# A Strassen operand moved from GpSimd to VectorE in small steps, and Sinkhorn steps and weight subtractions kept in different feature tiles

## The chip, the cores and the metric

The kernel runs on one core of one Trainium2 chip. The metric is the device time of one execution, in microseconds (us). Five engines work side by side, each in its own program order: TensorE (PE, with its weight loads PEld), VectorE (DVE), ScalarE (ACT), GpSimd (POOL) and SyncE (SP, which issues most DMAs).

## What is computed

Three layers in float32, one behind the other:

```
x   = mLSTM attention(q, k, v, gates)                 # 1536 tokens x 320
P   = exp(x @ w_gate - max)                           # 1536 x 8 experts
8 times: P /= row sums; P /= column sums; P *= N / E  # Sinkhorn
x1  = sum over e of P[:, e] * (relu(x @ w1[e]) @ w2[e])      # moe, every expert for every token
out = gate * (relu(x1 @ v1[e*]) @ v2[e*])             # moe2, one expert e* for each token
```

Precision is kept by splitting each float32 matrix into a high part (fp32r, a rounded copy) and a low part (the difference): `xh`, `xl`, `w1h`, `w1l`, `w2h`, `w2l`, `hh`, `hl`. A product is the sum of high-high, high-low and low-high matmuls.

## The kernel before

The first moe layer is a list of 25 items, written out by hand in `moe1`; an item is one expert on one block of tokens. Tokens lie in blocks 0, 1 and 2 of 512. Items 0 and 1 are expert 0 on the halves of block 0; items 2 to 7 are experts 1 to 6 on block 0; items 8 to 21 are experts 0 to 6 on blocks 1 and 2 in turn; items 22 to 24 are expert 7 on the three blocks. The attention layer is spread into items 0 to 3 by a counter of units (`bg_early`), so its twelve token tiles are computed between the matmuls of block 0.

Items 0 to 7 and 22 to 24 have a first stage of eight *feature tiles* (`s1_unit`, eight matmuls of 512 columns each into one of two PSUM banks named `s`). When the eight are done, ACT takes the relu (`hh`, L707) and DVE the low part (`hl`, L708); only then may the feature tile after next write that bank. The second stage (`s2_mm`, L713 to L715) has four token tiles of four pieces (six matmuls each); the last piece of a token tile is followed by an eviction on DVE (L742, or L740 where an accumulator is first written), which frees one of two banks.

Items 8 to 21 replace the first stage by Strassen's scheme with seven products (`s1_seven`). For these, each token block needs operands made once: the four combinations `th` with low parts `tl`, and a stacked remainder `ts`. `make_x(b)` makes them for blocks 1 and 2. The weight's combinations are made on POOL (`make_sums`, L561 to L567, into the tiles `sums` and `sumt`) and then split by ACT and DVE (`make_w`).

Three more streams run beside the matmuls. `split_chunk` turns a loaded piece of weight (`raw`, four buffers) into high part (ACT, L476) and low part (DVE or POOL, L482), and then lets SP issue the next load into the freed buffer; chunks 0 to `DVE_CHUNKS - 1` have the low part on DVE. `sinkhorn` is a generator whose sixteen half steps on DVE (L404 to L408, then L411 to L414), with an all-reduce on POOL between them, are taken at every second unit from unit 100. `fold_raw` (in item 5) scales the first four items' outputs by P and adds them up.

All work is recorded in program order; an engine runs its instructions strictly in that order and waits where a semaphore is not yet there.

The lines that give the moments, of the version before:

```
if newe and ft < 3 or n == 0 and ft in (2, 4, 6):          # L781: w2 split behind which feature tiles
    split_chunk()
...
if u % 2 == 1 and slow:                                    # L1379: a Sinkhorn half step
...
if n == EARLY and u % 2 == 1:                              # L1429: a fold step, EARLY = 5
    next(active[0], None)
elif EARLY <= n < SEVEN - 1 and (n, u) >= (EARLY, 2 * NF): # make_x, one step a unit, SEVEN = 8
```

A unit `u` counts two to a feature tile (0 to 15), and then one to a piece of the second stage (16 to 31).

## Time and profile before

| | us |
|---|---|
| three timed runs | 981.46, 984.47, 984.52 |
| median of them | 984.47 |
| the profiled execution's own time | 980.54 |
| its span, first to last instruction | 978.8 |
| busy in that span: PE, DVE, ACT, POOL | 938.5, 627.1, 470.9, 312.1 |

The profiled execution lies 0.9 us below the fastest timed run and 3.9 us below the median. Times of rows are counted from the start of the span. The items that the change touches lie at 198.5 to 229.9 us (item 4), 229.9 to 262.9 (item 5), 262.9 to 295.7 (item 6), 295.7 to 322.7 (item 7) and 322.7 to 351 (item 8, the first with seven products). A PE row's end is modelled: matmuls overlap, so the idle time shown before one is less than the distance that the stall adds between two starts.

### The profile page before, as it was taken

To read this page: it belongs to the slowest core of one execution; us is meant where nothing else is said; L and a number is where in the kernel's file an instruction comes from. 1 tells how busy PE (TensorE), PEld (TensorE's weight loads), DVE (VectorE), ACT (ScalarE), POOL (GpSimd) and SP (SyncE) were. 2 spreads that over 40 slices of the span, in tenths; PEclk is the share of its full clock that TensorE was granted. 3 is DMA by queue.
4 is the path that set the end of the run, shared out by engine and by line. 5 is a ranking of instruction groups with operands and counts; after the bars stand their busy time and mean duration, and the time that the engine had idled before them with its cause. 6 is when DMAs were issued, how large, how long until landed. Compare 5 with 4: busy or idle time off the path is not lost. (4 is left out here: it accounts for less than half of the span.)

```text
span 978.8 us, 17087 instructions
## 1 busy us (share of the span) xinstructions
PE 938.5 (96%) x6387; PEld 870.5 (89%) x6389; DVE 627.1 (64%) x1463; ACT 470.9 (48%) x936; POOL 312.1 (32%) x308
## 2 busy tenths in 40 slices
PE   8899989999989999999999999999999999899995
PEld 5888888877878999999999999999988987678995
DVE  8867765676765747474856747474535569874672
ACT  5655546334465446353646446353432135465662
POOL 3222311002537704225070704321221112225663
PEclk9999999999999999999999999999999999899998
DMA  9724431223233304031210304021270035587440
GB/s 196 180 43 109 101 79 44 76 64 119 58 107 86 109 1 130 1 93 38 73 58 5 125 2 130 1 91 50 77 301 28 22 96 148 169 231 226 123 127 20
DMA packets 93719, 91.39 MB, mean 93 GB/s; under 512 B 54845, under 2 KB 82495, under 8 KB 93632
## 3 DMA queue, kind: packets, MB, share of 16 engines
q1 hardware_dynamic: 91424, 83.50, 30.3%
q0 software_dynamic: 2208, 6.75, 2.2%
q8 instruction: 52, 0.85, 0.4%
q14 instruction: 35, 0.29, 0.1%
HBM read 86.29 MB, written 4.76 MB: 93 GB/s over the span
## 5 line engine op out<-in xcount | busy, mean ns | idle before, releaser
L713 PE MATMUL s<-w2h,hh 128*128 128x320 f32 x768 | 241.6, 315 | 1.1 <-DVE acc L742 1.0
L715 PE MATMUL s<-w2h,hl 128*128 128x320 f32 x768 | 238.8, 311 | 0.0
L714 PE MATMUL s<-w2l,hh 128*128 128x320 f32 x768 | 237.9, 310 | 0.0
L713 PEld LDWEIGHTS s<-w2h,hh 128*128 128x128 f32 x768 | 145.1, 189 | 2.6 <-DVE acc L742 1.6
L714 PEld LDWEIGHTS s<-w2l,hh 128*128 128x128 f32 x768 | 145.2, 189 | 0.6
L715 PEld LDWEIGHTS s<-w2h,hl 128*128 128x128 f32 x768 | 144.8, 188 | 0.7
L707 ACT ACTIVATE hh<-s 128x512 fp32r<-128x512 f32 (+1 forms) x88 | 49.1, 559 | 107.5 <-PE s L706 107.4
L615 PE MATMUL a<-th,w 128*128 128x256 f32 x392 | 100.0, 283 | 0.0
L708 DVE SCALAR_TENSOR_TENSOR hl<-s,hh 128x512 fp32r<-128x512 f32 (+1 forms) x88 | 56.2, 639 | 67.3 <-ACT hh L707 66.8
L615 PE MATMUL a<-ts,wx 96*128 96x256 f32 x336 | 95.3, 284 | 0.0
L478 POOL CAST w2h<-raw 128x960 fp32r<-128x960 f32 (+1 forms) x21 | 21.5, 1024 | 218.0 <-PE s L715 218.0
L742 DVE SCALAR_TENSOR_TENSOR acc<-s,probs,acc 128x320 f32<-128x320 f32 x72 | 39.6, 550 | 75.6 <-PE s L715 75.5
L615 PEld LDWEIGHTS a<-th,w 128*128 128x128 f32 x392 | 74.6, 190 | 0.0
L636 ACT COPY p<-a 128x256 f32<-128x256 f32 x56 | 20.9, 374 | 102.5 <-PE a L615 98.5
L615 PEld LDWEIGHTS a<-ts,wx 96*128 96x128 f32 x336 | 63.7, 189 | 0.0
L615 PE MATMUL a<-tl,w 128*128 128x256 f32 x224 | 63.0, 281 | 0.0
L482 POOL TENSOR_TENSOR w2l<-raw,w2h 128x960 fp32r<-128x960 f32 (+1 forms) x27 | 54.9, 2039 | 20.8 <-ACT w2h L476 19.1
L628 DVE SCALAR_TENSOR_TENSOR hl<-s,hh 128x256 fp32r<-128x256 f32 x112 | 46.8, 418 | 22.9 <-ACT hh L624 22.7
L624 ACT ACTIVATE hh<-a 128x256 fp32r<-128x256 f32 x112 | 43.1, 385 | 37.8 <-DVE a L631 32.3
L628 DVE SCALAR_TENSOR_TENSOR hl<-a,hh 128x256 fp32r<-128x256 f32 x112 | 47.6, 425 | 14.4 <-ACT hh L624 6.3
L247 POOL TENSOR_SCALAR_AFFINE_SELECT W<-W 128x512 f32<-128x512 f32 x24 | 17.7, 741 | 112.3 <-issue 88.9
L624 ACT ACTIVATE hh<-s 128x256 fp32r<-128x256 f32 x112 | 43.3, 387 | 8.3 <-DVE s L631 7.5
(360 smaller groups left out, 2381.6 us busy)
## 6 DMA issues: line engine op xcount, KB each, us to landing
raw<-in_moe_w_dram SPq DMA_DIRECT2D x30, 512.0 KB
raw<-in_moe_w_dram SPq DMA_DIRECT2D x30, 480.0 KB
raw<-in_moe_w_dram SPq DMA_DIRECT2D x39, 320.0 KB
raw<-in_moe_w_dram SPq DMA_DIRECT2D x40, 256.0 KB
wr<-in_moe_w_dram SPq DMA_DIRECT2D x8, 1024.0 KB
w2raw<-in_moe_w_dram SPq DMA_DIRECT2D x12, 640.0 KB
raw<-in_moe_w_dram SPq DMA_DIRECT2D x42, 128.0 KB
q<-in_q_dram SPq DMA_DIRECT2D x12, 160.0 KB
```

Source lines behind the costliest of these rows:

```text
L478: hi.tensor_copy(h, rv)
L482: eng.tensor_tensor(out=l, in0=rv, in1=f32(h), op=ALU.subtract)
L615: pe.matmul(bank, w, x, start=(first and n == 0), stop=(n == 3), skip_group_check=True)
L624: act.activation(out=hh[:, ft, h * HT:(h + 1) * HT], in_=p, func=AF.Relu)
L628: dve.scalar_tensor_tensor(out=hl[:, ft, c], in0=p, scalar=0.0, in1=f32(hh[:, ft, c]), op0=ALU.max, op1=ALU.subtract)
L636: act.copy(out=p1, in_=Bk[j])
L707: act.activation(out=hh[:, ft, 0:n], in_=p, func=AF.Relu)
L708: dve.scalar_tensor_tensor(out=hl[:, ft, 0:n], in0=p, scalar=0.0, in1=f32(hh[:, ft, 0:n]), op0=ALU.max, op1=ALU.subtract)
L713: pe.matmul(p[:, 0:DM], hh[:, ft, ts], w2h[:, ft, :], start=(ft == 0), stop=False)
L714: pe.matmul(p[:, 0:DM], hh[:, ft, ts], w2l[:, ft, :], start=False, stop=False)
L715: pe.matmul(p[:, 0:DM], hl[:, ft, ts], w2h[:, ft, :], start=False, stop=(ft == NF - 1))
L742: dve.scalar_tensor_tensor(out=acc[:, tt, 0:DM], in0=p[:, 0:DM], scalar=probs[:, tt, e:e + 1], in1=acc[:, tt, 0:DM], op0=ALU.mult, op1=ALU ...
```

## The change

Seven things change together.

1. In `sinkhorn`, the multiplication by N/E and the one by the reciprocal column sums become one instruction.
2. From item 3 on, the three w2 splits stand behind feature tiles 0, 2 and 4 instead of 0, 1 and 2.
3. No Sinkhorn half step is taken in the first eight units of item 4 (its feature tiles 0 to 3); the steps that are left run to the item's last unit.
4. Fold steps in item 5 are taken at every third unit of the first stage and at each of the first eight pieces of the second.
5. `make_x` runs on DVE and ACT alone, in twenty small steps. Block 1's are taken at odd units of items 5, 6 and the start of item 7; block 2's are taken in item 8, two behind each piece of its second stage. Its scratch (`xs`) and `raw_b` lie in the tile `sums`, which therefore is opened early.
6. `DVE_CHUNKS` goes from 39 to 42: item 7's three w2 low parts move from POOL to DVE.
7. `sums` and `sumt` become one tile, and `p1`, `u4`, `u2` become one tile `pu`.

```diff
@@ -410,8 +410,8 @@
-            dve.tensor_scalar_mul(out=cs[:, 0, :], in0=cs[:, 0, :], scalar1=float(N) / E)
-            dve.tensor_tensor(out=probs, in0=probs, in1=cs[:, 0, :].unsqueeze(1).to_broadcast([128, NT, E]), op=ALU.mult)
+            dve.scalar_tensor_tensor(out=probs, in0=probs, scalar=float(N) / E, in1=cs[:, 0, :].unsqueeze(1).to_broadcast([128, NT, E]),
+                                     op0=ALU.mult, op1=ALU.mult)
...
-    DVE_CHUNKS = 39
+    DVE_CHUNKS = 42
...
-        sx["tmp"] = tc.tile_pool(name="stm", bufs=1)
-        p = sx["tmpp"] = sx["tmp"].__enter__()
-        raw_b[0] = p.tile([128, TPB, DM], F32, name="raw_b")
...
         sx["wx"] = p.tile([128, 9, HF], F32R, name="wx")
-        sx["sm"] = p.tile([128, 3, HF], F32, name="sums")
-        sx["st"] = p.tile([128, 3, HF], F32, name="sumt")
...
+        sums = p.tile([128, 6, HF], F32, name="sums")
+        sx["sm"], sx["st"] = sums[:, 0:3], sums[:, 3:6]
+        pu = p.tile([128, 4, HT], F32, name="pu")
+        sx["p1"], sx["u4"], sx["u2"] = pu[:, 0], pu[:, 1], [pu[:, 2], pu[:, 3]]
+        sx["xs"] = sums.rearrange("p m f -> p (m f)").rearrange("p (x t) -> p x t", t=HT)
+        raw_b[0] = sums.rearrange("p m f -> p (m f)")[:, 0:TPB * DM].rearrange("p (t d) -> p t d", d=DM)
...
     def make_x(b):
...
+        w = sx["xs"]
+        xm, tt, xt, tm = w[:, 0:4], w[:, 4:8], w[0:64, 8:10], w[0:64, 10:12]
+        z, z4 = tm[0:32], xm[0:32]
         th, tl, ts = sx["th", b], sx["tl", b], sx["ts", b]
...
+        def sub(o, x, y, op=ALU.subtract):
+            dve.tensor_tensor(out=o, in0=x, in1=y, op=op)
         act.copy(out=tm, in_=two(f32(xh[b][64:128, 2, :])))
-        yield
-        pool.tensor_tensor(out=xm.rearrange("p a h t -> p a (h t)"), in0=f32(xh[b][:, 0:2, :]), in1=f32(xl[b]), op=ALU.add)
...
-        pool.tensor_tensor(out=xt, in0=two(f32(xh[b][0:64, 2, :])), in1=tm, op=ALU.add)
-        yield
-
-        def combine(o, a1, a2, b1, b2, first):
-            return [(o[:, first], a2, a1), (o[:, first + 2], b2, a2), (o[:, first + 1], b2, o[:, first]), (o[:, first + 3], b1, o[:, first + 1])]
-        for o, x, y in combine(tt, xm[:, 0, 0], xm[:, 0, 1], xm[:, 1, 0], xm[:, 1, 1], 0):
-            pool.tensor_tensor(out=o, in0=x, in1=y, op=ALU.subtract)
-            yield
-        act.copy(out=th, in_=tt)
-        act.copy(out=z[:, 0:2], in_=xt[32:64])
-        yield
-        dve.tensor_tensor(out=tl, in0=tt, in1=f32(th), op=ALU.subtract)
-        yield
-        for o, x, y in combine(z, xt[0:32, 0], xt[0:32, 1], z[:, 0], z[:, 1], 2):
-            pool.tensor_tensor(out=o, in0=x, in1=y, op=ALU.subtract)
-            yield
+        sub(xm[:, 0:2], two(f32(xh[b][:, 0, :])), two(f32(xl[b][:, 0, :])), ALU.add)
+        yield
+        sub(xm[:, 2:4], two(f32(xh[b][:, 1, :])), two(f32(xl[b][:, 1, :])), ALU.add)
+        yield
+        sub(xt, two(f32(xh[b][0:64, 2, :])), tm, ALU.add)
+        act.copy(out=z, in_=xt[32:64])
+        yield
+        sub(tt[:, 0:3:2], xm[:, 1:4:2], xm[:, 0:2])
+        act.copy(out=th[:, 0:3:2], in_=tt[:, 0:3:2])
+        yield
+        sub(tt[:, 1], xm[:, 3], tt[:, 0])
+        yield
+        sub(tt[:, 3], xm[:, 2], tt[:, 1])
+        act.copy(out=th[:, 1:4:2], in_=tt[:, 1:4:2])
+        yield
+        sub(z4[:, 0], xt[0:32, 1], xt[0:32, 0])
+        yield
+        sub(z4[:, 2], z[:, 1], xt[0:32, 1])
+        yield
+        sub(z4[:, 1], z[:, 1], z4[:, 0])
+        yield
+        sub(tl[:, 0:2], tt[:, 0:2], f32(th[:, 0:2]))
+        yield
+        sub(tl[:, 2:4], tt[:, 2:4], f32(th[:, 2:4]))
+        yield
+        sub(z4[:, 3], z[:, 0], z4[:, 1])
+        yield
+        parts = [(0, 1, xt[0:32, 0:1]), (1, 3, z), (3, 5, z4[:, 0:2]), (5, 7, z4[:, 2:4])]
         for q in (0, 64):
-            act.copy(out=ts[q:q + 32, 0], in_=xt[0:32, 0])
-            act.copy(out=ts[q:q + 32, 1:7], in_=z)
-            yield
-        dve.tensor_tensor(out=ts[32:64, 0], in0=xt[0:32, 0], in1=f32(ts[0:32, 0]), op=ALU.subtract)
-        dve.tensor_tensor(out=ts[32:64, 1:7], in0=z, in1=f32(ts[0:32, 1:7]), op=ALU.subtract)
-        yield
+            for x0, x1, a in parts:
+                act.copy(out=ts[q:q + 32, x0:x1], in_=a)
+                if q:
+                    sub(ts[32:64, x0:x1], a, f32(ts[0:32, x0:x1]))
+                yield
@@ -778,7 +777,7 @@
                 assert not left_over
                 for ft in range(NF):
                     s1_unit(t0, nt, ft, lambda: bg(n, 2 * ft))
-                    if newe and ft < 3 or n == 0 and ft in (2, 4, 6):
+                    if newe and (ft < 3 if n < EARLY - 2 else ft in (0, 2, 4)) or n == 0 and ft in (2, 4, 6):
                         split_chunk()
             if n == CLASSIC - 1:
-                close_w()
+                close_x()
                 open_late()
             work = make_w() if nxt and nsv else None
+            x2 = make_x(2) if n == SEVEN else None
...
                     f()
+                if n == SEVEN:
+                    for _ in range(2):
+                        next(x2, None)
                 if work is not None:
                     next(work, None)
...
+        MID = sum(2 * NF + 4 * nt for _, nt, _ in ITEMS[:EARLY - 1])
 
         def bg_early(u):
             for g in list(active):
                 if next(g, "end") == "end":
                     active.remove(g)
-            if u % 2 == 1 and slow:
+            if slow and u % 2 == 1 and not MID <= u < MID + NF:
                 if next(slow[0], "end") == "end":
                     slow.pop(0)
...
-                    xs.extend((make_x(1), make_x(2)))
+                    xs.append(make_x(1))
                 return
             if n == EARLY and u == 0:
                 emit_const2()
-            if n == EARLY and u % 2 == 1:
-                next(active[0], None)
-            elif EARLY <= n < SEVEN - 1 and (n, u) >= (EARLY, 2 * NF):
-                if next(xs[0], "end") == "end" and len(xs) > 1:
-                    xs.pop(0)
-                if (n, u) == (SEVEN - 2, 2 * NF + 4 * TPB - 1):
-                    for g in xs:
-                        drain(g)
-            if n == SEVEN - 1 and u == 0:
-                open_w()
+            if n == EARLY and u < 2 * NF + 8:
+                if u >= 2 * NF or u % 3 == 1:
+                    next(active[0], None)
+            elif EARLY <= n < SEVEN and u % 2 == 1 and u >= 7:
+                next(xs[0], None)
+            if n == SEVEN - 1 and u == 7:
+                drain(xs[0])
```

On DVE, in item 4's first feature tiles, before (`hl` marks the end of a feature tile, L482 is a w2 split, L404 to L413 are Sinkhorn):

```order
L708 SCALAR_TENSOR_TENSOR hl<-s_2159,hh 128x512
L482 TENSOR_TENSOR w2l<-raw,w2h 128x960
L404 TENSOR_REDUCE sk<-probs 128x12
L405 TENSOR_SCALAR sk<-sk 128x12
L406 RECIPROCAL sk<-sk 128x12
L407 TENSOR_TENSOR probs<-probs,sk 128x96
L408 TENSOR_REDUCE cs<-probs 128x8
L708 SCALAR_TENSOR_TENSOR hl<-s_2180,hh 128x512
L482 TENSOR_TENSOR w2l<-raw,w2h 128x960
L411 TENSOR_SCALAR cs<-cs 128x8
L412 RECIPROCAL cs<-cs 128x8
L413 TENSOR_SCALAR cs<-cs 128x8
```

On the same engine at the same place after the change:

```order
L707 SCALAR_TENSOR_TENSOR hl<-s_2157,hh 128x512
L482 TENSOR_TENSOR w2l<-raw,w2h 128x960
L707 SCALAR_TENSOR_TENSOR hl<-s_2172,hh 128x512
L707 SCALAR_TENSOR_TENSOR hl<-s_2183,hh 128x512
L482 TENSOR_TENSOR w2l<-raw,w2h 128x960
L707 SCALAR_TENSOR_TENSOR hl<-s_2199,hh 128x512
L707 SCALAR_TENSOR_TENSOR hl<-s_2210,hh 128x512
L482 TENSOR_TENSOR w2l<-raw,w2h 128x640
L404 TENSOR_REDUCE sk<-probs 128x12
L405 TENSOR_SCALAR sk<-sk 128x12
L406 RECIPROCAL sk<-sk 128x12
L407 TENSOR_TENSOR probs<-probs,sk 128x96
```

Split and Sinkhorn half step stood in one feature tile three times; now they meet once, behind feature tile 4.

On ACT, in item 6 before, between the relus (`hh`) of feature tiles 2, 3 and 4 (`ts` is block 1's stacked remainder):

```order
L707 ACTIVATE hh<-s_2753 128x512
L476 CAST w2h<-raw 128x640
L550 CAST ts_2307<-xt 32x256
L551 CAST ts_2307<-z 32x1536
L550 CAST ts_2307<-xt 32x256
L551 CAST ts_2307<-z 32x1536
L707 ACTIVATE hh<-s_2771 128x512
L707 ACTIVATE hh<-s_2786 128x512
```

On ACT in item 6 after the change, from feature tile 3 on:

```order
L706 ACTIVATE hh<-s_2744 128x512
L706 ACTIVATE hh<-s_2756 128x512
L476 CAST w2h<-raw 128x640
L534 CAST th_2281<-sums 128x2x256
L706 ACTIVATE hh<-s_2773 128x512
L706 ACTIVATE hh<-s_2785 128x512
L706 ACTIVATE hh<-s_2797 128x512
```

The four `ts` copies are gone from between the relus; one `th` copy of 512 columns stands there.

On DVE, in item 8's second stage, where there were only the evictions (L740, now L739), after the change:

```order
L739 TENSOR_SCALAR acc<-s_3358,probs 128x320
L519 TENSOR_TENSOR sums<-xh_67,xl_70 128x512 x2
L519 TENSOR_TENSOR sums<-xh_67,sums 64x512
L519 TENSOR_TENSOR sums<-sums 128x2x256
L519 TENSOR_TENSOR sums<-sums 128x256 x2
L519 TENSOR_TENSOR sums<-sums 32x256 x2
L739 TENSOR_SCALAR acc<-s_3402,probs 128x320
L519 TENSOR_TENSOR sums<-sums 32x256
L519 TENSOR_TENSOR tl_2285<-sums,th_2284 128x512 x2
L519 TENSOR_TENSOR sums<-sums 32x256
L739 TENSOR_SCALAR acc<-s_3439,probs 128x320
```

Behind the third eviction stand four more, which make the low rows of `ts`; block 2's whole operand now stands between item 8's evictions and item 9's first products.

## Rows read from the trace of the kernel before

**Rows 1.** The page, part 1: busy us of each engine (share of the span) xinstructions.
```profile
PE 938.5 (96%) x6387; PEld 870.5 (89%) x6389; DVE 627.1 (64%) x1463; ACT 470.9 (48%) x936; POOL 312.1 (32%) x308
```
**Rows 2.** TensorE's waits, first stages of items 4, 5; second of 5; item 6: total, times, longest.
```profile
PE s L698 <- DVE hl L708: 1.9, 3, 1.0
...
PE s L698 <- DVE hl L708: 2.4, 2, 2.2
...
PE s L713 <- DVE acc L742: 1.0, 1, 1.0
...
PE s L698 <- DVE hl L708: 3.1, 2, 2.3
```
**Rows 3.** Timeline of PE, items 4 and 5: start us, duration us, instruction [idle before <-releaser].
```profile
203.51 0.39 PE L705 MATMUL s<-xh,w 128*128 128x512 f32 x1
203.74 0.39 PE L706 MATMUL s<-xh,w 128*128 128x512 f32 x1
205.12 0.50 PE L698 MATMUL s<-xh,w 128*128 128x512 f32 x1 [0.99 <-DVE hl L708]
...
243.88 0.39 PE L698 MATMUL s<-xh,w 128*128 128x512 f32 x1
```
**Rows 4.** Timeline of DVE in item 4.
```profile
203.10 0.24 DVE L404 TENSOR_REDUCE sk<-probs 128x12 f32<-128x96 f32 x1
...
204.38 0.68 DVE L708 SCALAR_TENSOR_TENSOR hl<-s,hh 128x512 fp32r<-128x512 f32 x1
204.98 1.15 DVE L482 TENSOR_TENSOR w2l<-raw,w2h 128x960 fp32r<-128x960 f32 x1
206.04 0.17 DVE L411 TENSOR_SCALAR cs<-cs 128x8 f32<-128x8 f32 x1
...
206.86 0.68 DVE L708 SCALAR_TENSOR_TENSOR hl<-s,hh 128x512 fp32r<-128x512 f32 x1
```
**Rows 5.** Timeline of POOL in item 5: the first instruction of `make_x`.
```profile
235.98 3.09 POOL L531 TENSOR_TENSOR xm<-xh,xl 128x1024 f32<-128x1024 f32 x1
```
**Rows 6.** Timeline of DVE in items 5 and 6.
```profile
236.74 2.69 DVE L724 SCALAR_TENSOR_TENSOR acc<-acc,probs 128x320 f32<-128x320 f32 x1
...
240.68 0.54 DVE L724 SCALAR_TENSOR_TENSOR acc<-raw_b,probs,acc 128x320 f32<-128x320 f32 x1
...
242.92 0.69 DVE L708 SCALAR_TENSOR_TENSOR hl<-s,hh 128x512 fp32r<-128x512 f32 x1 [0.64 <-ACT hh L707]
...
244.77 0.69 DVE L708 SCALAR_TENSOR_TENSOR hl<-s,hh 128x512 fp32r<-128x512 f32 x1 [0.70 <-ACT hh L707]
...
250.16 2.39 DVE L482 TENSOR_TENSOR w<-raw,w 128x1024 fp32r<-128x1024 f32 x1 [0.56 <-ACT w L476]
...
291.31 0.42 DVE L553 TENSOR_TENSOR ts<-xt,ts 32x256 fp32r<-32x256 f32 x1
```
**Rows 7.** Timeline of ACT in item 6.
```profile
269.69 0.40 ACT L550 CAST ts<-xt 32x256 fp32r<-32x256 f32 x1
...
271.80 1.46 ACT L551 CAST ts<-z 32x1536 fp32r<-32x1536 f32 x1
273.28 1.09 ACT L707 ACTIVATE hh<-s 128x512 fp32r<-128x512 f32 x2
```
**Rows 8.** Timeline of POOL in item 7.
```profile
299.35 6.04 POOL L482 TENSOR_TENSOR w2l<-raw,w2h 128x960 fp32r<-128x960 f32 x3 [12.36 <-ACT w2h L476]
...
310.66 1.29 POOL L561 TENSOR_TENSOR sumt<-raw 96x512 f32<-96x512 f32 x1
```
**Rows 9.** Timeline of DVE in items 7 and 8 and at the start of item 9.
```profile
320.63 0.68 DVE L594 TENSOR_TENSOR w<-sums,w 128x512 fp32r<-128x512 f32 x1
...
341.67 0.55 DVE L740 TENSOR_SCALAR acc<-s,probs 128x320 f32<-128x320 f32 x1 [0.51 <-PE s L715]
...
348.71 0.55 DVE L740 TENSOR_SCALAR acc<-s,probs 128x320 f32<-128x320 f32 x1 [2.97 <-PE s L715]
351.48 0.43 DVE L631 TENSOR_TENSOR s<-s,p 128x256 f32<-128x256 f32 x1 [2.22 <-PE s L615]
```

More of the change, by code (lines that the diff above doesn't have):

```diff
@@ L498, in open_x @@
             sx["ts", b] = p.tile([128, 7, HT], F32R, name=f"ts{b}")
-        sx["tmp"] = tc.tile_pool(name="stm", bufs=1)
-        p = sx["tmpp"] = sx["tmp"].__enter__()
-        raw_b[0] = p.tile([128, TPB, DM], F32, name="raw_b")
-    def open_w():
-        sx["tmp"].__exit__(None, None, None)
-        sx["wp"] = tc.tile_pool(name="swp", bufs=1)
-        p = sx["pool"] = sx["wp"].__enter__()
-        sx["wx"] = p.tile([128, 9, HF], F32R, name="wx")
-        sx["sm"] = p.tile([128, 3, HF], F32, name="sums")
-        sx["st"] = p.tile([128, 3, HF], F32, name="sumt")
-        sx["p1"] = p.tile([128, HT], F32, name="p1")
-        sx["u4"] = p.tile([128, HT], F32, name="u4")
-        sx["u2"] = [p.tile([128, HT], F32, name=f"u2{j}") for j in range(2)]
@@ L515, in close_w @@
-    def close_w():
-        sx["wp"].__exit__(None, None, None)
+        sx["wx"] = p.tile([128, 9, HF], F32R, name="wx")
+        sums = p.tile([128, 6, HF], F32, name="sums")
[4 more added lines that the diff above has]
+        raw_b[0] = sums.rearrange("p m f -> p (m f)")[:, 0:TPB * DM].rearrange("p (t d) -> p t d", d=DM)
@@ L517, in close_w, with close_x @@
+    def close_x():
         sx["xp"].__exit__(None, None, None)
     def make_x(b):
-        p = sx["tmpp"]
-        xm = p.tile([128, 2, 2, HT], F32, tag="xm", name="xm")
-        tt = p.tile([128, 4, HT], F32, tag="tt", name="tt")
-        xt = p.tile([64, 2, HT], F32, tag="xt", name="xt")
-        tm = p.tile([64, 2, HT], F32, tag="tm", name="tm")
-        z = p.tile([32, 6, HT], F32, tag="z", name="z")
+        w = sx["xs"]
+        xm, tt, xt, tm = w[:, 0:4], w[:, 4:8], w[0:64, 8:10], w[0:64, 10:12]
+        z, z4 = tm[0:32], xm[0:32]
```

## The prediction

> **What bounds the kernel now.** The page's first part comes first: TensorE is busy for 96% of the span, the next engine for 64% [rows 1]. So only time in which TensorE stands still, or runs matmuls that it need not, can be won, and the change removes no matmul. The waits of TensorE come second, asked for by item. In items 4, 5 and 6 it waits for `hl` (the low part of the relu, on VectorE) in the first stages for 1.9, 2.4 and 3.1 us, and for one eviction in item 5's second stage for 1.0 us [rows 2]; nothing else there. The timeline of PE gives the true size: two matmuls start 0.23 us apart while each is drawn 0.39 us long, so a wait costs 0.16 us more than the idle time shown; 203.74 to 205.12 is 1.38, 0.23 of it normal, so 1.15 for a wait shown as 0.99 [rows 3]. With 0.16 for each of the eight waits, item 4 loses 1.9 + 3 x 0.16 = 2.4, item 5 2.4 + 2 x 0.16 = 2.7 and 1.0 + 0.16 = 1.2, item 6 3.1 + 2 x 0.16 = 3.4: 9.7 us. That is the most that these edits can return here.
>
> The timelines of VectorE and ScalarE then say why `hl` is late. An undisturbed feature tile takes 1.85 us (242.92 to 244.77), and the `hl` at 242.92 ends at 243.61, while the matmul that may then overwrite its bank starts at 243.88 [rows 3, 6]. So there is 0.27 us of slack: whatever delays one `hl` by more stops TensorE two feature tiles later.
>
> **The change part by part.**
>
> Item 4, first stage. `hl` takes a slot of 0.60 us (204.38 to 204.98), a split of 960 columns 1.06 (204.98 to 206.04), the first half of a Sinkhorn step 1.28 (203.10 to 204.38), the second half 0.82 (206.04 to 206.86) [rows 4]. Before, `hl` + split + first half = 2.94 us against a period of 1.85, three feature tiles running: hence the 2.4. After, feature tiles 0 and 2 hold 0.60 + 1.06 = 1.66 and 1 and 3 hold 0.60: all fit. Feature tile 4 holds the short split (640 columns, 1.06 x 2/3 = 0.71) and a first half: 0.60 + 0.71 + 1.28 = 2.59, or 0.74 late, less 0.27 of slack: about 0.5, taken as 0.6 since the split also waits for ScalarE's copy. From there on a half step of 1.28 with `hl` is 1.88, just even. The merged multiplication saves one instruction of 0.17 us (as L411) in each second half, off the path. Gain 2.4 - 0.6 = 1.8; if feature tile 4 came out even, 2.4.
>
> Item 5, first stage. The long wait is the 2.2 of rows 2, and its cause is one row: a fold instruction that took 2.69 us instead of 0.54 [rows 6], started at 236.74 beside the first `make_x` instruction on GpSimd, 235.98 to 239.07 [rows 5]. After the change GpSimd runs no `make_x`, so the fold takes 0.54, and every third unit it stands where no split does, except in feature tile 0. There split and fold still meet as now: the short wait of 2.4 - 2.2 + 0.16 = 0.4 stays. Gain 2.3.
>
> The Trainium skill (SBUF — State Buffer, Who interferes with whom) has a rule for this: a VectorE instruction with two SBUF inputs and a GpSimd instruction that reads SBUF exclude each other, and the second waits for all of the first. The trace agrees: the fold ends 0.4 us after GpSimd's instruction.
>
> Item 5, second stage. A w1 split took 2.39 us [rows 6], beside GpSimd's `make_x`; the next sizes alone are 1.06 for 960 columns [rows 4]. After, VectorE has in the first eight pieces seven folds (0.5 each), three w1 splits (1.06 x 1024/960 = 1.13 each) and an eviction (0.55): 7.4 us, against eight pieces of 0.88 (two evictions eight pieces apart are 348.71 - 341.67 = 7.04 [rows 9]). It is 0.4 behind, and a bank has four pieces to be freed. Gain 1.2.
>
> Item 6. ScalarE makes the four `ts` copies in one piece from 269.69, and the next relu starts at 273.28 [rows 7]: 3.6 us in a period of 1.85. Its `hl` and the next are late, which is the 3.4. After, the fullest feature tile holds on ScalarE a relu, a w2 copy and one `th` copy, on VectorE `hl`, the short split and a subtraction of 256 columns at 0.42 [rows 6]: 0.60 + 0.71 + 0.42 = 1.73. Gain 3.4.
>
> Item 7. Here the change adds work to a stage without waits. Behind feature tile 3 stand three `ts` subtractions of 512 columns (0.68 each alone [rows 9], 0.60 a slot): `hl` + 1.8 = 2.4, or 0.55 late, less 0.27: 0.3 lost. Then the third split, now on VectorE, meets the first weight sum on GpSimd, which waits for the same subtractions because its output overlays their inputs. Its price: alone 0.71; beside GpSimd up to 2.39/1.13 times that, 1.5 [rows 6]. I take half of the difference, 0.4, of which some 0.3 reaches TensorE, since `hl` behind it has just lost its slack. Loss 0.6; bounds 0 (if ScalarE's relu were the later anyway) and 1.7 (both in full, and the next `hl` too).
>
> By the Trainium skill's rule (SBUF — State Buffer, Who interferes with whom, as above) the split would wait out the whole sum that has begun, at most its 1.29 us [rows 8]; with all of that on TensorE the loss in this item would be 1.6 and the sum 7.1. No row shows this pair.
>
> Queued behind that split is SP's load of the last weight quarter. Before, GpSimd's splits ended at 305.39 and the sum that reads this quarter started at 310.66 without a wait [rows 8], so the load lands in under 5.3 us. After, the split ends some 12.7 us into the item and the sum's turn comes at 16.4 (10.6 when the subtractions are done, four sums of 1.29, and 0.6 for contention): 0 to 1.6 us late, before a `make_w` that has some slack. I take 0, and keep 1 as the bound.
>
> Item 8. Block 2's operand is sixteen VectorE instructions, nine of 512 columns (0.60 a slot) and seven of 256 (0.42 less the overlap, 0.34): 7.8 us. They start behind the eviction at 341.67, with two more evictions between (0.92) and about 0.5 for results that are needed at once: done at 342.13 + 9.2 = 351.3. Item 9's first sum on VectorE starts at 351.48 [rows 9], and TensorE reads only the first `ts` row in its first product, at about 350.6; that row is made before the last three, at 349.6. It fits by less than 1 us. Cover: TensorE's second-stage pieces, in which VectorE stands idle for 2.97 us before an eviction [rows 9]. Without it the whole 7.8 would show. I take 0; bounds 0 and a loss of 1.
>
> The rest. Items 3 and 22 have later splits too: in 3 they stand differently among attention's instructions (0, bounds 0.5 either way); in 22 GpSimd does three splits in 6.04 [rows 8] with 1.85 x 3 = 5.5 us left behind the last one's copy: 0. The loads that splits release start up to 3.7 us later, at least a whole second stage ahead of their use. The shared tiles `pu` and `sums` add no wait between parts that do not overlap, since the program's waits in items 10 to 21 are the same as before: 0.
>
> Sum: 1.8 + 2.3 + 1.2 + 3.4 - 0.6 = 8.1 us. Low end: 8.1 - 0.3 (item 4) - 1.1 (item 7) - 1 (load) - 1 (item 8) - 0.5 (item 3) = 4.2; high end: 8.1 + 0.6 + 0.6 + 0.5 = 9.8. Against the profiled execution, 980.54 - 8.1 = 972.4. The timed runs' median lies 3.9 higher, which by itself gives 984.47 - 8.1 = 976.4. I forecast 975, nearer to the second, as medians are compared.
>
> **The rivals.**
>
> Less comes back. Feature tile 4 of item 4, item 7 and the start of item 9 each turn into a wait: gain 4 or less, 977 to 981. For it: three places that fit by under 1 us. Against: each has its own slack, and they would have to fail together.
>
> More comes back. The stalls that go are those of over 2 us; if timed runs have longer ones than the profiled execution (their median is 3.9 higher), 10 to 13 return: 969 to 972. No row shows it.
>
> No change. The edits only move the stalls: VectorE takes over block 1's operand in items 5 to 7, up to 7.8 us as for block 2, and every feature tile that was relieved fills up again: 983 to 985. Against: only in feature tile 4 of item 4 and in 3 of item 7 does the count exceed 1.85.
>
> Slower. Block 2's subtractions in item 8 are stretched as the fold was, by 2.69/0.54 = 5 [rows 6], if GpSimd reads SBUF beside them: 7.8 becomes 39, item 9 waits 30 us, and the time is near 1000. At three times it is 15.6 longer, less 1 of slack and 8.1 of gain: 6.5 slower, 990. The point that decides is a stretch of (8.1 + 1)/7.8 + 1 = 2.2. For it: the next work of GpSimd in program order is item 9's weight sums, which read SBUF. Against: after the change their output overlays block 2's scratch, so they must wait until it has been read; GpSimd should stand idle there.
>
> **How the numbers follow.** The forecast has 0.67 (971 to 978.5, its own range), less 0.13, more 0.06, no change 0.07, slower 0.07. The range 970.5 to 980.5 takes the forecast, most of "less" and half of "more": 0.8. A difference under 0.3%, 2.9 us, is about what a measurement of this kernel cannot tell from none. Faster by more: 0.67 + 0.13 + 0.06 = 0.86; the same 0.07; slower 0.07.
>
> **What the profile after would show.** Right: item 4 with one wait for `hl` of about 0.5 us, item 5 with one of 0.2, item 6 with none; the folds at 0.54 all through; a new wait in item 7 under 1 us; item 9's first product without a wait, and VectorE's last `ts` subtraction about at its start. Wrong: a wait for `ts` or for a weight part at the start of items 8 or 9; subtractions of 512 columns that take over 1 us in item 8; or all this as said and an equal time, which would mean that the waits removed were not on the path.

## The result, and the profile after

| | before | after |
|---|---|---|
| median (lowest to highest), four runs each | 982.97 (979.87 to 984.52) | 972.02 (970.89 to 973.88) |
| ratio, 95% interval | | 0.9894 [0.9861, 0.9928] |
| profiled execution, its span | 980.54, 978.8 | 973.88, 972.2 |

The change is faster by 1.1%, with an interval of 0.7 to 1.4%. Two later comparisons of the same two kernels gave 0.9921 [0.9892, 0.995] and 0.9903 [0.9875, 0.9931]. The forecast was 975 us, from a sum of 8.1 us.

The page's first part of the kernel after, to be laid beside [rows 1]: GpSimd has lost 30 us of work, VectorE has gained only 6, and TensorE, 96% busy as before, has the same matmuls in a shorter span.

```profile
span 972.2 us, 17087 instructions
...
PE 937.0 (96%) x6389; PEld 869.5 (89%) x6389; DVE 633.2 (65%) x1484; ACT 472.4 (49%) x946; POOL 281.8 (29%) x285
```

TensorE's waits of the kernel after, first for items 4 to 6 (196 to 286 us), then for items 7 to 9 (285 to 375 us): total, times, longest.

```profile
PE s L697 <- DVE hl L707: 1.2, 3, 0.7
...
PE s L697 <- DVE hl L707: 0.5, 1, 0.5
PE s L712 <- DVE acc L741: 0.5, 1, 0.5
```

The 8.4 us of waits of [rows 2] have become 1.2, and item 7 has two new ones. To count what a wait costs without the modelled ends, I take the distance between the first matmuls of two items, from the timeline of PE. The last column is a later variant in which TensorE has no wait left in these items (called "early parts" below), so it shows what each item takes undisturbed.

| us | before | after | difference | forecast | undisturbed |
|---|---|---|---|---|---|
| item 4 | 31.49 | 29.51 | -1.98 | -1.8 | 28.80 |
| item 5 | 32.94 | 29.20 | -3.74 | -3.5 | 28.84 |
| item 6 | 32.85 | 29.74 | -3.11 | -3.4 | 29.00 |
| item 7 | 27.00 | 28.60 | +1.60 | +0.6 | 27.10 |
| items 8 and 9 | 42.60 | 42.60 | 0.00 | 0 | 42.61 |
| sum | 166.88 | 159.65 | -7.23 | -8.1 | 156.35 |

So 8.8 us come back in items 4 to 6, and 1.6 are given away in item 7 (1.5 and 2.0 in two later profiles of the changed kernel, where item 7 takes 28.51 and 28.99 us). Outside these items the two profiled executions differ too, in ways that nearly cancel. The execution of before reached item 4 1.8 us later; it has a stretch of 3.4 us ahead of it with the clock at its lower level, which the execution after does not have. Windows of the kernel before (first TensorE's busy time and its matmuls; the granted clock is the third number from the end; 0.50 is the level of 1.2 GHz):

```profile
139.00:140.70 1.70, 1.26 (x10) 1.27 (x11) 0.48 (x3) 0.00 (x0) 0.00 (x0) 1.00 0.86 248
140.70:144.10 3.40, 3.40 (x15) 3.40 (x14) 3.04 (x6) 0.43 (x1) 0.00 (x0) 0.50 0.36 83
```

And from item 22 to the end the execution after takes 2.6 us longer, 271.3 us against 268.7. Two later profiles of the changed kernel take 267.8 and 270.7 us there, so this stretch differs between executions of one program by as much.

### The profile page after: what moved, and what is told of

It is laid out like the page before. It is cut to its first block, busy times and chain, and to the rows that moved or that the text cites. A ratio compares the mean times of both kernels' runs of the same rounds, so it can differ in the third digit from the quotient of the medians.

```text
span 972.2 us, 17087 instructions
## 1 busy us (share of the span) xinstructions
PE 937.0 (96%) x6389; PEld 869.5 (89%) x6389; DVE 633.2 (65%) x1484; ACT 472.4 (49%) x946; POOL 281.8 (29%) x285
## 5 line engine op out<-in xcount | busy, mean ns | idle before, releaser
L635 ACT COPY pu<-a 128x256 f32<-128x256 f32 x56 | 20.9, 374 | 91.8 <-PE a L614 87.6
L482 POOL TENSOR_TENSOR w2l<-raw,w2h 128x960 fp32r<-128x960 f32 (+1 forms) x24 | 48.9, 2036 | 11.0 <-ACT w2h L476 9.3
```

The source lines that it names most:

```text
L482: eng.tensor_tensor(out=l, in0=rv, in1=f32(h), op=ALU.subtract)
```

## The experiments

**The changed kernel again**, with no edit.

> The changed kernel as it is, for a narrower interval and for the spread between executions. Theory (the gain is the 7.3 us of waits that its profile no longer shows in items 4 to 7): ratio near 0.9925, time some 7 us under the kernel before. Rival (the 11 us between the first medians is real and has a further source outside items 4 to 9): ratio near 0.989. If the mean granted clock of the executions differs between the two kernels, the difference beyond 7 us is in stretches at the lower clock level; if it does not, it is elsewhere.

Measured: 974.9 us against 981.31, ratio 0.9921 [0.9892, 0.995]. Items 4 to 7 take 116.96 us (117.05 in the first profile), so the 7 us are a property of the program, as the theory had it. This execution reached item 4 six us later than the other (202.74 against 196.68), and the windows show where: in the first 28 us, while inputs still arrive. The row of this execution, and under it that of the first profile:

```profile
13.00:28.00 15.00, 14.45 (x66) 13.08 (x66) 7.51 (x20) 6.88 (x11) 2.83 (x11) 0.50 1.07 213
```
```profile
13.00:28.00 15.00, 11.65 (x86) 9.78 (x85) 12.98 (x33) 8.93 (x15) 2.84 (x11) 1.00 1.04 211
```

The same 15 us ran at the lower level in one and at the upper in the other: 66 matmuls instead of 86. Items 4 to 9 of these two profiles and of the profile before hold no stretch at the lower level, so the lengths in the table are free of it.

The expectation also asked whether the mean granted clock differs between the two kernels. It hardly does here, 0.9877 for the kernel before and 0.9884 for the changed one, but it spreads between executions, from 0.979 to 0.997, and the time goes with it. An estimate from the 169 timed runs of all the experiments, with a level for each kernel and each set of comparisons and one common slope: a run is 0.68 us longer for each 0.001 that its mean clock is lower. At equal clock, by this fit, the changed kernel is 6.9 us (5.9 to 8.0) faster here and 7.8 (6.2 to 9.3) in the later comparison. Both agree with the 7.2 us of the items, so no second source is needed. The fit was made after the results were known, and it would also take out what a stall costs by lowering the clock.

**Only the moments (edits 1 to 4).** The kernel before, with the merged multiplication and the new moments of splits, Sinkhorn steps and folds; `make_x` stays on GpSimd, in its own scratch.

```diff
...
-            if n == EARLY and u % 2 == 1:
+            if n == EARLY and u < 2 * NF + 8 and (u >= 2 * NF or u % 3 == 1):
                 next(active[0], None)
-            elif EARLY <= n < SEVEN - 1 and (n, u) >= (EARLY, 2 * NF):
+            if EARLY <= n < SEVEN - 1 and (n, u) >= (EARLY, 2 * NF):
```

> The kernel before with the moments alone changed: merged multiplication, w2 splits behind feature tiles 0, 2, 4 from item 3 on, Sinkhorn paused in item 4, fold steps at the new units; the Strassen operand stays on GpSimd and in items 5 and 6. Theory (three separate causes): item 4's wait for hl falls from 1.9 us to about 0.4, item 5 keeps a wait of about 2 us because a fold still runs beside GpSimd's first instruction, its eviction wait stays at 1 us or more, item 6 keeps its 3.1 us; gain 1.5 to 2.5 us. Rival (the moments are all of it): items 4 to 6 without waits over 0.5 us, gain about 7 us.

Measured: ratio 1.0027 [0.9996, 1.0058], and items 4 to 7 in 130.08 us, 5.8 longer than before. Item 4 gained its 2.0 (29.50). Item 5 took 37.78. Its waits (first row), and what stood on VectorE and GpSimd ahead of the longest:

```profile
PE s L713 <- DVE acc L742: 5.5, 2, 5.3
```
```profile
252.72 1.76 DVE L482 TENSOR_TENSOR w<-raw,w 128x1024 fp32r<-128x1024 f32 x1
254.40 3.36 DVE L724 SCALAR_TENSOR_TENSOR acc<-acc,probs 128x320 f32<-128x320 f32 x1
...
258.26 0.55 DVE L742 SCALAR_TENSOR_TENSOR acc<-s,probs,acc 128x320 f32<-128x320 f32 x1
```
```profile
252.41 2.64 POOL L547 TENSOR_TENSOR z<-z 32x256 f32<-32x256 f32 x2
255.02 2.38 POOL L531 TENSOR_TENSOR xm<-xh,xl 128x1024 f32<-128x1024 f32 x1
```

The fold of 0.54 us [rows 6] took 3.36: it ends 0.36 us behind GpSimd's instruction (255.02 + 2.38 = 257.40), and the eviction is queued behind it. Neither gain expected held. The moments alone push the folds into the second stage, where GpSimd runs the operand; edit 4 needs edit 5. Item 7 lost another 2.38 us at an eviction. Rows of GpSimd, of ACT and of VectorE ahead of it:

```profile
315.45 1.29 POOL L563 TENSOR_TENSOR raw<-raw 96x512 f32<-96x512 f32 x1
```
```profile
316.78 1.05 ACT L590 CAST wx<-raw 96x1024 fp32r<-96x1024 f32 x1 [4.74 <-POOL raw L563]
```
```profile
317.86 1.22 DVE L598 TENSOR_TENSOR wx<-raw,wx 32x1024 fp32r<-32x1024 f32 x1 [3.64 <-ACT wx L590]
```

ScalarE's copy waits for a weight sum of GpSimd, VectorE's subtraction for the copy, and the eviction stands behind the subtraction. The sums come late because GpSimd still makes the three w2 low parts, which now stand behind feature tiles 0, 2 and 4: the last one ends 12.2 us into the item, 9.7 before [rows 8]. So edit 2 needs edit 6 as well. Both long waits were followed by a stretch at the lower clock level:

```profile
258.50:261.90 3.40, 3.04 (x11) 3.04 (x12) 1.90 (x3) 0.00 (x0) 0.00 (x0) 0.50 0.00 0
319.90:323.30 3.40, 3.40 (x14) 3.40 (x15) 3.34 (x4) 2.57 (x2) 0.31 (x1) 0.50 0.73 207
```

The 25 matmuls in them start some 0.12 us further apart than at the upper level (0.27 instead of 0.147), so I estimate that 3 of the 5.8 us are the clock's. At equal clock the timed runs are 2.0 us (0.8 to 3.1) slower than before by the fit above.

**The old moments of splits and Sinkhorn** in the changed kernel (edits 2 and 3 undone).

```diff
-                    if newe and (ft < 3 if n < EARLY - 2 else ft in (0, 2, 4)) or n == 0 and ft in (2, 4, 6):
+                    if newe and ft < 3 or n == 0 and ft in (2, 4, 6):
...
-            if slow and u % 2 == 1 and not MID <= u < MID + NF:
+            if slow and u % 2 == 1:
```

> The changed kernel with w2 splits behind feature tiles 0, 1, 2 again and Sinkhorn not paused. Theory: item 4's three waits for hl come back (1.9 us in total as shown, 2.4 lost), item 5 stays under 0.6; item 6's new wait (0.7 us as shown) goes, since the th copy on ScalarE no longer stands behind a split; item 7 loses 0.5 us less; together 0.3 us slower to 0.7 us faster than the changed kernel. Rival (the engine alone matters, not the moments): item 4 without waits, the time that of the changed kernel in every item.

Measured: ratio 0.9944 [0.9913, 0.9975]; items 4 to 7 in 117.81 us, 0.8 longer. Item 4 loses 2.1 us in three waits (2.4 before the change). But the wait of 0.86 us in item 6 is gone, and the eviction wait in item 7 is down to 0.14. By lengths the new moments are worth 1.8 us in item 4 and 0.4 in item 5, and cost 0.7 in item 6 and 0.6 in item 7. The 0.8 lies just outside the range that was expected; the timed runs do not part this variant from the changed kernel (0.9944 against 0.9921, with intervals that overlap).

**A GpSimd instruction beside the folds.** The changed kernel with one sum more, whose result nobody reads, of the size of the old `make_x` instruction.

```diff
             if n == EARLY and u == 0:
                 emit_const2()
+                w = sx["xs"].rearrange("p x t -> p (x t)")
+                pool.tensor_tensor(out=w[:, 1536:2560], in0=f32(xh[1][:, 0:2, :]).rearrange("p a t -> p (a t)"),
+                                   in1=f32(xl[1]).rearrange("p a t -> p (a t)"), op=ALU.add)
```

> The changed kernel with one more GpSimd instruction at the start of item 5: an addition of 1024 columns that reads SBUF twice, as the first instruction of the operand did before; nothing waits for it and nothing reads its result. Theory (an SBUF-reading GpSimd instruction holds up a VectorE instruction with two SBUF inputs): a fold or a split in item 5's first stage takes 1.5 to 2.7 us instead of 0.54 or 1.16, a wait for hl of 1 to 2.2 us comes back in item 5, the time is 1 to 2.3 us longer than that of the changed kernel. Rival (the long fold was late for another reason): all VectorE durations in item 5 as in the changed kernel, no wait over 0.3 us.

Measured: a new wait of TensorE in item 5's first stage, 1.16 us between starts; items 4 to 7 in 118.89 us, which is within what was expected. Of the 1.9 us more, 1.4 are in item 5 and 0.5 at the eviction in item 7. The sum met a split of 640 columns this time, which alone takes 0.83. Timeline of VectorE, then of GpSimd:

```profile
237.69 2.27 DVE L482 TENSOR_TENSOR w2l<-raw,w2h 128x640 fp32r<-128x640 f32 x1
```
```profile
236.82 2.45 POOL L1434 TENSOR_TENSOR sums<-xh,xl 128x1024 f32<-128x1024 f32 x1
```

GpSimd is done at 239.27; with 0.83 behind that the split would end at 240.10, and it ends at 239.96.

**GpSimd beside block 2's operand**: the slower rival made on purpose. Eleven sums that read SBUF, with a result that nobody reads, in item 8's second stage.

```diff
...
+                if n == SEVEN and x == 0:
+                    for _ in range(11):
+                        pool.tensor_tensor(out=sx["dum"], in0=acc[:, t0, 0:DM], in1=acc[:, t0, 0:DM], op=ALU.add)
                 if n == SEVEN:
                     for _ in range(2):
                         next(x2, None)
```

> The changed kernel with eleven GpSimd additions of 320 columns in item 8, which read SBUF twice, start when the first eviction of its second stage is done, and whose result nobody reads. Theory (the forecast's slower rival, built on purpose: GpSimd reading SBUF stretches block 2's subtractions): the subtractions of 512 columns take 1.2 us or more instead of 0.68, those together end 4 to 8 us later, item 9's first products wait 3 to 7 us for ts, items 4 to 7 stay as in the changed kernel; slower than it by 3 to 7 us. Rival (the place has room enough, or the two engines do not hinder each other): durations of 0.4 and 0.68 as in the changed kernel, no wait over 0.3 us at item 9.

Measured: items 8 and 9 in 47.40 us instead of 42.60, ratio 0.9959 [0.9936, 0.9982]. Of VectorE, GpSimd and TensorE's waits in item 8:

```profile
336.33 4.63 DVE L520 TENSOR_TENSOR sums<-sums 128x512 f32<-128x512 f32 x5
```
```profile
333.63 11.63 POOL L802 TENSOR_TENSOR dum<-acc 128x320 f32<-128x320 f32 x11 [9.81 <-DVE acc L740]
```
```profile
PE a L615 <- ACT ts L552: 2.0, 1, 2.0
PE s L713 <- DVE acc L740: 1.5, 1, 1.5
```

Five sums take 4.63 us that take 2.26 in the changed kernel (below), and both an eviction and item 9's first product wait. The loss of 4.8 us lies in the range expected; TensorE's wait for `ts` is shorter than expected (2.0 us instead of 3 to 7), and the eviction has a part of the loss.

**The operand on GpSimd, at the new moments.** Everything of the change stays, but the sums and differences that make `xm`, `xt`, `tt` and `z` are on GpSimd.

```diff
-        sub(xm[:, 0:2], two(f32(xh[b][:, 0, :])), two(f32(xl[b][:, 0, :])), ALU.add)
+        sub(xm[:, 0:2], two(f32(xh[b][:, 0, :])), two(f32(xl[b][:, 0, :])), ALU.add, eng=pool)
...
-        sub(z4[:, 3], z[:, 0], z4[:, 1])
+        sub(z4[:, 3], z[:, 0], z4[:, 1], eng=pool)
```

> The changed kernel with the additions and subtractions of the operand on GpSimd again, at the new moments; its tl and ts rows stay on VectorE. Theory (the engine matters as much as the moment): in item 8 ten GpSimd instructions of 0.7 to 1.3 us make about 9.5 us before the last z, so item 9 waits 3 to 6 us; in items 5 to 7 folds and splits beside GpSimd are stretched and 0.5 to 3 us of waits come back; slower than the changed kernel by 3 to 8 us. Rival (only the moments matter): the same time as the changed kernel within 1 us in items 4 to 9.

Measured: 974.32 us, ratio 0.9916 [0.9883, 0.995]; items 4 to 7 in 116.27 us, 0.8 *shorter* than on VectorE (item 6 has no wait and takes 28.76), items 8 and 9 0.8 longer, of which 0.35 stand in the second profile of the changed kernel too (42.95). My theory fell. The timeline of GpSimd, and one row of VectorE, show why this is not the old picture:

```profile
244.94 2.18 POOL L519 TENSOR_TENSOR sums<-xh,xl 128x512 f32<-128x512 f32 x1 [6.62 <-ACT w L476]
252.91 1.31 POOL L519 TENSOR_TENSOR sums<-xh,xl 128x512 f32<-128x512 f32 x1 [5.79 <-DVE acc L723]
```
```profile
244.25 0.54 DVE L723 SCALAR_TENSOR_TENSOR acc<-sums,probs,acc 128x320 f32<-128x320 f32 x1
```

Before, the first sum started at 235.98, as soon as GpSimd had nothing else to do [rows 5]. Here it starts 9 us later, in the second stage, 0.15 us behind the end of the fold that reads the second token tile of `raw_b` (the view names a copy of ScalarE for this wait, but that ended at 244.55, and GpSimd's queue waited for VectorE until 244.84). The second one waits for a fold (L723) by name: the scratch lies over `raw_b`, which the folds read. A fold still took 1.62 us beside the first sum, but there it had time.

**The same without the shared memory.** As the last kernel, with `raw_b` in other tiles, so that the scratch no longer lies over it.

```diff
...
-        raw_b[0] = sums.rearrange("p m f -> p (m f)")[:, 0:TPB * DM].rearrange("p (t d) -> p t d", d=DM)
+        r3 = pu.rearrange("p m f -> p (m f)")[:, 0:3 * DM].rearrange("p (t d) -> p t d", d=DM)
+        r1 = p.tile([128, DM], F32, name="raw_b3")
+        raw_b[0] = [r3[:, 0], r3[:, 1], r3[:, 2], r1]
...
```

> Like the kernel with the operand's sums on GpSimd at the new moments, except that the four item-3 outputs (raw_b) lie in other tiles (three in pu, one in a new tile), so that the operand's scratch no longer overlays what the folds read. There, GpSimd's first two sums started at 244.94 and 252.91 us, the second behind a fold on VectorE, and items 4 to 7 took 116.3 us. Theory (the shared memory paced GpSimd): without it GpSimd runs the two sums as soon as its small constants are made, at 236 to 242 us, in item 5's first stage; one fold there takes over 1.2 us instead of 0.55, TensorE stands still 0.7 to 1.6 us for hl, items 4 to 7 take 117.0 to 117.9 us. Rival (the place in the program or another wait paces it): the sums stay at 245 and 253 us and the items at 116.0 to 116.6.

Measured: 978.16 us, ratio 0.9954 [0.9926, 0.9981]; items 4 to 7 in 119.73 us, 3.5 longer than with the overlay. Of GpSimd, of VectorE, and TensorE's waits in items 4 to 7:

```profile
236.37 3.17 POOL L521 TENSOR_TENSOR sums<-xh,xl 128x512 f32<-128x512 f32 x2
```
```profile
238.29 1.60 DVE L725 SCALAR_TENSOR_TENSOR acc<-acc,probs 128x320 f32<-128x320 f32 x1
```
```profile
PE s L714 <- DVE acc L743: 2.6, 2, 2.2
PE s L699 <- DVE hl L709: 2.0, 4, 0.9
```

Both sums run at 236 us, the fold beside them takes 1.60 instead of 0.55, and TensorE stands 1.10 us for `hl`: the theory held for the first stage. It was too small by the second stage, where the rest of the operand now meets the folds and an eviction costs 2.35 more.

**The copies apart.** The kernel before, with three steps of nothing behind each pair of `ts` copies, to price item 6's cause by itself.

```diff
             act.copy(out=ts[q:q + 32, 1:7], in_=z)
             yield
+            yield
+            yield
+            yield
```

> The kernel before with three empty steps behind each pair of ts copies, so that the two pairs on ScalarE stand in two different feature tiles; nothing else changes. Theory (item 6's 3.4 us come from 3.6 us of copies in one piece on ScalarE): item 6's wait for hl falls from 3.1 us to 0.5 to 1.5, as each pair of 1.8 us still overfills its tile by 0.5; items 4 and 5 as in the kernel before; gain 1.5 to 2.5 us. Rival (the wait is VectorE's, from the ts subtraction of 1.74 us or from GpSimd beside it): item 6's wait stays at 2.5 us or more.

Measured: item 6 in 29.54 us instead of 32.85, so the four copies in one piece cost 3.3 us: the 3.4 of the prediction, and more than the 1.5 to 2.5 expected here. Item 4 (31.47 us), item 7 (27.21) and the long stand-still of item 5 repeat the one profile that there is of the kernel before. The time moved less: ratio 0.9982 [0.9953, 1.001], items 4 to 7 1.7 shorter. Item 5, which the edit does not touch, took 34.40 instead of 32.94. Windows of this kernel around the long wait in item 5:

```profile
236.00:240.30 4.30, 2.11 (x8) 1.43 (x8) 4.30 (x4) 2.17 (x4) 3.30 (x5) 0.98 0.81 231
240.30:243.50 3.20, 3.19 (x8) 2.52 (x9) 2.21 (x4) 0.00 (x0) 0.00 (x0) 0.50 0.47 145
```

The stand-still itself was as long as in the kernel before (2.34 us), but here the eight matmuls behind it ran at the lower level, 0.43 us apart instead of 0.23, eight times 0.2 us, which is the 1.5 us. In the profile of before the same stretch is at 1.00.

**Early parts.** The changed kernel with its own leftovers moved: splits back behind feature tiles 0, 1, 2 from item 4 on, Sinkhorn paused for six units instead of eight, the folds from unit 7 on, and block 1's operand finished in item 6, so that item 7 starts clean.

```diff
-                    if newe and (ft < 3 if n < EARLY - 2 else ft in (0, 2, 4)) or n == 0 and ft in (2, 4, 6):
+                    if newe and (ft in (0, 2, 4) if n == EARLY - 2 else ft < 3) or n == 0 and ft in (2, 4, 6):
...
-            if slow and u % 2 == 1 and not MID <= u < MID + NF:
+            if slow and u % 2 == 1 and not MID <= u < MID + 6:
...
-                if u >= 2 * NF or u % 3 == 1:
+                if u >= 2 * NF or u >= 7 and u % 2 == 1:
                     next(active[0], None)
-            elif EARLY <= n < SEVEN and u % 2 == 1 and u >= 7:
+            elif EARLY <= n < SEVEN - 1 and u >= 7 and (u % 2 == 1 or n > EARLY and u >= 2 * NF):
                 next(xs[0], None)
-            if n == SEVEN - 1 and u == 7:
+            if n == SEVEN - 1 and u == 0:
```

> The changed kernel with its four left waits taken away: w2 splits behind feature tiles 0, 1, 2 again in items 4 to 7, Sinkhorn and folds only behind feature tile 3 and later, block 1's operand finished in item 6's second stage. Theory (each of these waits comes from two things in one feature tile): the waits of 0.5 in item 4, 0.3 in item 5, 0.9 in item 6, 0.7 and 0.6 in item 7 go; items 4 to 7 take 114 us instead of 117, the time is about 3 us under the changed kernel. Rival (VectorE is full, waits only move): items 4 to 7 take 116 to 118 us, other waits of the same sum appear, most likely in item 6's second stage.

Measured: 971.54 us, ratio 0.9886 [0.985, 0.9923]. Items 4 to 7 take 113.74 us, and the list of TensorE's waits from 190 to 375 us is empty. To see whether that is worth its 3.3 us, it ran once more beside the changed kernel.

> The same kernel as the variant with the weight splits behind feature tiles 0, 1, 2, a shorter pause and block 1's operand done in item 6, beside the changed kernel in the same call. Items 4 to 7 took 113.7 us in its first profile and 117.0 in the changed kernel's. If that is worth 3.3 us in the timed runs too, its ratio to the kernel before lies 0.003 below that of the changed kernel here, near 0.989 against 0.992; if something later gives it back, the two ratios are equal.

> The changed kernel as it is, for the comparison with the variant beside it in this call: a ratio to the kernel before of 0.992 (0.989 to 0.995), items 4 to 7 in 117.0 us.

Measured: 970.4 us, ratio 0.9895 [0.9857, 0.9932], for the variant; 972.84, 0.9903 [0.9875, 0.9931], for the changed kernel. In the two profiles items 4 to 7 take 113.72 and 117.54 us and the spans 968.9 and 972.1, so nothing gives the gain back there. The medians differ by 2.4 us the same way, but the two ratios by only 0.0008, with intervals that overlap almost wholly: taken as they are, the timed runs do not show the variant to be faster than the changed kernel. The mean granted clock of its six runs was lower, though, 0.9878 against 0.9908. At equal clock, by the fit above, it is 3.2 us (1.4 to 5.1) faster, which agrees with the 3.8 of the items, and 10.2 (8.7 to 11.6) and 11.0 (9.5 to 12.5) faster than the kernel before, where the table has 10.5.

## Why the prediction was right, and where its steps were off

**What bounds the kernel** was read rightly: TensorE's waits in items 4 to 6 were on the path, and taking them away shortened the span by their size. The correction for modelled ends was a little small. Against the undisturbed items, items 4, 5 and 6 lost 2.7, 4.1 and 3.9 us before, 10.6 in all, where I had 9.7.

**Item 4** kept one wait at feature tile 7, 0.53 us between starts; forecast 0.6. In "early parts" its splits stand behind feature tiles 0, 1 and 2, as before the change, and it has no wait: the pause of the Sinkhorn steps (edit 3) is enough for item 4's gain, and the later splits (edit 2) are not needed there. **Item 5** kept one of 0.33 (forecast 0.4), and its folds take 0.54 or 0.55; one follows the third split too (237.30 and 238.04), which I had not seen, and costs nothing. The reason I gave, that GpSimd runs no `make_x`, is true of the changed kernel, but it is not what was needed. With the sums on GpSimd the items are just as short as long as the scratch lies over `raw_b`; without that the stalls return. What item 5's part of the gain rests on is *when* the operand is made. In the kernel before, nothing held GpSimd back, and it ran ahead of its place in the program into the first stage. The change holds the operand back twice: on VectorE by its place in the queue, and by the memory that it shares with the folds. The second is enough, also on GpSimd; the first without the second was not tried.

**Item 6.** The term that I took whole, 3.4, returned 3.1 with a wait of 0.86 us left over. I had added up VectorE's load for a feature tile, 1.73, and named ScalarE's three pieces without adding them, and I had left out the handover between the two. Timeline of ACT, then of VectorE, in item 6 of the kernel after:

```profile
267.20 0.62 ACT L534 CAST th<-sums 128x512 fp32r<-128x512 f32 x1 [1.23 <-DVE sums L519]
267.73 1.30 ACT L706 ACTIVATE hh<-s 128x512 fp32r<-128x512 f32 x2
```
```profile
266.01 0.82 DVE L482 TENSOR_TENSOR w2l<-raw,w2h 128x640 fp32r<-128x640 f32 x1
266.75 0.42 DVE L519 TENSOR_TENSOR sums<-sums 128x256 f32<-128x256 f32 x1
268.35 0.69 DVE L707 SCALAR_TENSOR_TENSOR hl<-s,hh 128x512 fp32r<-128x512 f32 x1 [1.18 <-ACT hh L706]
```

The split stands ahead of the subtraction, the `th` copy waits for the subtraction, and the relu stands behind the copy: ScalarE is idle for 1.23 us, and `hl` comes at 268.35. With the third split two feature tiles earlier (old moments, early parts) this wait is gone, and also with the subtraction on GpSimd, where no split stands ahead of it.

**Item 7** is the mis-sized term: 0.6 lost by forecast, 1.60 measured. Its first part has the size that I gave, 0.69, but partly by luck. All of it is from the three `ts` subtractions (1.89 us, 2.63 from `hl` to `hl` where I had 2.4), for which I had 0.3: TensorE's matmul at 296.87 waits for the `hl` that ends at 296.82, behind them. The third split, 1.19 us beside GpSimd's first sum, for which I had another 0.3, cost TensorE nothing: the `hl` behind it ends at 298.53, and the matmul two feature tiles on starts at 298.82 without a wait. GpSimd's sum ends at 297.24, 0.83 behind that is 298.07, and the split ends at 297.93. The Trainium skill (SBUF — State Buffer, Who interferes with whom) has the rule that the two exclude each other, and that the second waits for all of the first; the trace agrees to 0.14 us. What I had not followed is the sum that starts later. Rows of PE, of GpSimd, of ACT and of VectorE in item 7:

```profile
296.87 0.50 PE L697 MATMUL s<-xh,w 128*128 128x512 f32 x1 [0.53 <-DVE hl L707]
...
298.82 0.39 PE L697 MATMUL s<-xh,w 128*128 128x512 f32 x1
```
```profile
295.72 1.52 POOL L560 TENSOR_TENSOR sums<-raw 128x512 f32<-128x512 f32 x1 [59.12 <-ACT hh L706]
...
303.21 2.16 POOL L562 TENSOR_TENSOR raw<-raw 96x512 f32<-96x512 f32 x1
```
```profile
305.40 1.05 ACT L589 CAST wx<-raw 96x1024 fp32r<-96x1024 f32 x1 [2.95 <-POOL raw L562]
```
```profile
294.21 1.89 DVE L519 TENSOR_TENSOR ts<-sums,ts 32x512 fp32r<-32x512 f32 x3
296.13 0.69 DVE L707 SCALAR_TENSOR_TENSOR hl<-s,hh 128x512 fp32r<-128x512 f32 x1
296.74 1.19 DVE L482 TENSOR_TENSOR w2l<-raw,w2h 128x640 fp32r<-128x640 f32 x1
297.85 0.68 DVE L707 SCALAR_TENSOR_TENSOR hl<-s,hh 128x512 fp32r<-128x512 f32 x1
...
302.48 1.73 DVE L593 TENSOR_TENSOR w<-raw,w 128x1024 fp32r<-128x1024 f32 x1 [0.24 <-ACT w L587]
306.49 1.22 DVE L597 TENSOR_TENSOR wx<-raw,wx 32x1024 fp32r<-32x1024 f32 x1 [2.27 <-ACT wx L589]
307.74 0.55 DVE L741 SCALAR_TENSOR_TENSOR acc<-s,probs,acc 128x320 f32<-128x320 f32 x1
```

GpSimd waits for the subtractions because its output overlays their inputs (its queue waits for VectorE until 295.53, where the second of them has ended; the view names a later relu), and three of its first six sums meet VectorE and grow by 1.5 us in all; its sixth sum then ends at 305.37, ACT's copy waits 2.95 us for it, VectorE's subtraction 2.27 for the copy, and the eviction behind that comes too late: 0.65 us between starts of matmuls, 1.03 in a later profile. I had asked only whether the weight's load would be late for these sums, which it was not. In "early parts", where the subtractions stand in item 6, the first sum starts 1.7 us earlier in the item, none of the six grows, the sixth ends 3.4 us earlier, and item 7 takes 27.10 us. The bound of 1.7 held in two of the three profiles of the changed kernel (1.60 and 1.51) and not in the third (1.99).

**Item 8** came out at nothing, as forecast, and by as little as I had said. Timeline of VectorE, then of GpSimd, in item 8 of the kernel after:

```profile
332.67 0.55 DVE L739 TENSOR_SCALAR acc<-s,probs 128x320 f32<-128x320 f32 x1 [0.51 <-PE s L714]
333.14 1.28 DVE L519 TENSOR_TENSOR sums<-xh,xl 128x512 f32<-128x512 f32 x2
...
334.94 2.26 DVE L519 TENSOR_TENSOR sums<-sums 128x512 f32<-128x512 f32 x5
...
340.28 2.22 DVE L519 TENSOR_TENSOR ts<-sums,ts 32x256 fp32r<-32x256 f32 x4
342.60 0.43 DVE L630 TENSOR_TENSOR s<-s,pu 128x256 f32<-128x256 f32 x1
```
```profile
342.04 1.63 POOL L560 TENSOR_TENSOR sums<-raw 128x512 f32<-128x512 f32 x1 [17.96 <-DVE ts L519]
```

The last `ts` difference ends at 342.50, and VectorE's next instruction for item 9 starts at 342.60. GpSimd had been idle for 17.96 us before its next sum, waiting for the scratch, as the argument against the slower rival said. With GpSimd awake the rival comes true: 4.8 us slower in items 8 and 9.

**The rivals.** "No change" and "slower" fell by the profile. "Less comes back" named three places: item 7 cost more than forecast, item 4 no more than the sum had for it, and the start of item 9 nothing. "More comes back" had for it that the timed runs gained 7.8, 9.5 and 10.4 us by the three ratios, against 7.2 in the items. At equal clock the excess all but goes: 6.9 and 7.8 in the two later comparisons. The first comparison can't be put so, since the clock of its runs of before is not on record; its four runs of the changed kernel had a mean of 0.9905, nearer to the 0.9908 of the last one than to the 0.9884 of the second. Rows speak for one way in which a longer execution can come from a wait: a stretch at the lower level followed a long wait in the kernel with the copies apart and, twice, in the one with the moments alone. Whether it does so often in executions of before stays open.

## What to carry to other kernels

Add up a slot not only for each engine but along the handovers: an instruction that waits for another engine's small step holds everything queued behind it, here a relu behind a copy, and an eviction behind a weight subtraction. A helper engine with no data to wait for runs ahead of its place in the program and meets the work of others there; giving its scratch the memory that those others still read is a pacing tool, and the pieces of such a change may be worth nothing, or less, one by one. Measure each stage between first matmuls of the items, against a variant without waits, when whole executions spread by more than the effect; and compare executions at equal mean clock, where the clock is on record.

## What the runs showed of the hardware that was not expected

The same program took 6 us longer to item 4 in one execution than in another, because 15 us of its start ran at the lower clock level (66 matmuls instead of 86). A wait of 2.34 us was followed by eight matmuls at the lower level in one profile (granted clock 0.50) and by matmuls at the upper level in another (1.00). Where a VectorE and a GpSimd instruction met, GpSimd's grew too: a sum of 512 columns took 1.52, 1.76, 2.16 and 2.18 us instead of 1.30. Where VectorE's had begun first, GpSimd's ended 1.14 to 1.19 us behind VectorE's end, as if it too had waited for all of it: 297.24 behind 296.10, 305.37 behind 304.21, and, with the operand's sums on GpSimd, 247.12 behind 245.93, where a split ended.
